# The receptance weights of the first unit split into two parts, with another written order of the work

## The chip, the cores and the metric

The kernel runs on one core of a Trainium2 chip. The core has five engines that run at the same time, each through its own queue in order: PE (matrix multiplication), DVE (vector), ACT (scalar functions), POOL (GpSimd) and SP, which here issues the transfers. The metric is the device time of one execution in microseconds (us). The kernel before takes 607.31 us, the median of three runs (607.2 to 607.88).

## The reference

Two layers. The first is causal attention in a window: 8 batches, 8 heads, 576 tokens, 64 values a head; each token sees itself and the 63 tokens before it. Its output x (8 x 576 x 512) goes into the second layer:

```
x_prev = x moved by one token
xk = mu_k * x + (1 - mu_k) * x_prev
xr = mu_r * x + (1 - mu_r) * x_prev
k  = relu(xk @ w_k)                       # 512 x 1024
v  = (k * k) @ w_v                        # 1024 x 512
r  = 1 / (1 + exp(-(xr @ w_r)))           # 512 x 512
out = r * v
```

All tensors come as 64-bit numbers for the weights and 32-bit for the rest; the result is 32-bit.

## The kernel before, in words

**Units.** The 4608 tokens are cut into NU = 9 units of 512 tokens. Each unit runs through attention (`scores`, `soften`, `flip`, `values`), the mixes `xr` and `xk` (function `mix`), and the three products (`r_units`, `k_units`, `v_units`). The features of x stand on the partitions in NC = 4 chunks c of 128.

**Two ways to multiply.** A 32-bit factor is either kept whole, and a product is one 32-bit matmul of `xm` with `whole`; or it is split into a high part (a rounded copy) and a low part (the rest, a subtraction), and a product is three faster matmuls: high by high, high by low, low by high, of `xs` with `ws`. The function `direct` decides by the letters in `DIRECT`, and only for the first unit (u = 0): with "rk" the products with w_r and w_k are whole there. All other units, and w_v always, use the split factors. So the split of w_r and w_k is needed anyway, but before only from the second unit on.

**Weights.** `decode` turns each piece of 128 x 512 weights (n = 0 to 3 are w_r) from two 32-bit words into one 32-bit number: `sign` (ACT), `clamp` (POOL or DVE), `shift`, `top` and `low` (DVE). The result is a tile `wt` or, where it is used whole, half of a pair tile `whole`. `first_part` writes the high part `ws[:, 0]` (ACT or POOL), `second_part` subtracts and writes the low part `ws[:, 1]` (POOL or DVE).

**Mixes.** `mix` makes one chunk of xr or xk: `diff` (a scaled x_prev, on ACT, POOL or DVE), `blend` (DVE) and, where the factor is split, `high` (ACT or POOL) and `low` (POOL or DVE). The pieces that are whole write to a tile `xm`; the split ones have a scratch tile `d` and a tile `xs`.

**The order.** Every step is a `Piece` with a number. `play` plans which piece runs next on which engine. The table `ORDER` gives, for each of PE, DVE, ACT, POOL and SP, the numbers of the first pieces in the order in which the engine runs them; the rest follows by keys. While the planner's clock is under `BOUND`, a piece on POOL is also tied to the last DVE piece marked `port` that the planner started before it: the POOL instruction then waits on a semaphore until that DVE instruction is done (`Engine.behind`, `add_manual_dep` with the reason "port"). Nearly all instructions are issued by one helper, `issue`, so the profile has line L168 for them.

**Attention in the head of the program.** The first unit's attention goes in groups of two tiles `pr`. The scores are multiplied (`qk` or `qks`), the probabilities `pr` are made by DVE and ACT, multiplied by the reciprocal row sums `rs` on POOL or DVE, turned by PE (matmul with `ident`, called a flip, four to a tile), copied to `pt`, and multiplied with `v`. Two such groups give one chunk xT of x, from which `mix` works.

Of the kernel before, what the change touches and what calls it, by code (L numbers as in the profile page):

```python
# [47 lines left out]
GATES = 1  # L48
LATER = (4,)

DIRECT = "rk"
SPLIT = (-9, -47)
WHOLE = 859

# [34 lines left out]

ORDER = {  # L90
    "PE": (
        509, 510, 535, 531, 566, 533, 559, 561, 557, 555, 590, 563, 1502, 1509, 1516, 1523, 588, 586, 645, 614,
        1503, 1510, 612, 1524, 1517, 610, 667, 616, 1511, 1525, 1518, 1504, 1505, 1526, 1512, 1519, 1530, 1531,
        1538, 1532, 1539, 1540, 1546, 1547, 1554, 1533, 1548, 1541, 720, 1562, 1555, 1556, 1570, 1549, 1563, 1571,
        1557, 1564, 742, 1578, 1586, 1579, 1572, 1565, 1580, 1581, 1594, 1587, 1588, 689, 690, 1573, 1589, 1595,
        1604, 1596, 1614, 1605, 1624, 1625, 1626, 1615, 1606, 1607, 764, 765, 1597, 1598, 1627, 1599, 1616, 1628,
        1617, 1608, 1609, 1600, 1618, 771, 793, 1619, 1620, 1629, 1610, 1630, 1621, 1601, 1611, 1631, 1674, 1680,
        1681, 1682, 1686, 1675, 1692, 1676, 1677, 1683, 1693, 1698, 1694, 1706, 1695, 1707, 1708, 1714, 1709, 1715,
        1716, 1699, 1717, 1722, 1723, 1730, 1724,
    ),  # L100
    "DVE": (
        6, 7, 511, 513, 517, 521, 515, 525, 527, 523, 519, 8, 9, 529, 544, 536, 548, 540, 538, 550, 546, 542, 19,
        532, 20, 552, 567, 554, 575, 571, 581, 579, 577, 569, 573, 40, 21, 1487, 599, 591, 605, 31, 595, 593, 601,
        583, 32, 603, 597, 584, 33, 589, 1489, 23, 607, 646, 654, 648, 48, 658, 660, 49, 656, 650, 50, 652, 64, 55,
        65, 1491, 668, 66, 674, 56, 57, 676, 1493, 1495, 58, 72, 1497, 88, 662, 89, 682, 90, 1499, 73, 74, 80, 672,
        81, 680, 82, 678, 96, 104, 1501, 1508, 105, 670, 106, 1529, 97, 119, 98, 1522, 120, 664, 1515, 121, 666,
        122, 1537, 721, 128, 112, 729, 727, 113, 725, 731, 114, 733, 723, 735, 129, 684, 60, 130, 136, 137, 138,
        686, 144, 743, 747, 688, 1561, 745, 751, 145, 749, 146, 753, 757, 755, 100, 737, 52, 1553, 691, 152, 153,
        692, 159, 1569, 160, 738, 759, 739, 154, 161, 763, 162, 156, 741, 761, 164, 1635, 1585, 1593, 766, 168, 769,
        169, 170, 176, 767, 1640, 177, 1645, 84, 1650, 178, 772, 1655, 778, 794, 780, 782, 784, 802, 786, 808, 1648,  # L110
        180, 776, 806, 796, 1660, 774, 800, 1602, 804, 1612, 1632, 76, 1653, 1670, 1665, 1622, 798, 788, 1673, 1668,
        792, 1685, 790, 810, 813, 811, 814, 812, 1679, 1697,
    ),
    "ACT": (
        5, 514, 518, 512, 516, 522, 526, 524, 528, 17, 545, 537, 541, 539, 549, 547, 551, 543, 534, 29, 560, 562,
        582, 558, 556, 574, 576, 568, 570, 572, 580, 578, 600, 564, 602, 592, 598, 604, 606, 594, 587, 596, 46, 615,
        62, 655, 54, 34, 649, 613, 651, 659, 611, 661, 647, 70, 617, 657, 86, 1494, 78, 1496, 653, 1498, 94, 59,
        102, 1527, 1506, 1520, 677, 1528, 669, 673, 1507, 1513, 683, 118, 1521, 671, 126, 1534, 1514, 1535, 1542,
        110, 1536, 1543, 679, 1544, 681, 123, 134, 675, 142, 728, 1550, 730, 107, 732, 1558, 150, 1551, 99, 1559,
        131, 139, 1552, 726, 1560, 722, 1566, 724, 736, 1582, 744, 750, 746, 734, 147, 75, 1583, 758, 748, 158,  # L120
        1567, 756, 1568, 754, 693, 752, 1574, 1584, 1590, 694, 1575, 1591, 155, 166, 1576, 163, 1592, 1634, 174,
        1639, 768, 1644, 1649, 1654, 1651, 1646, 115, 179, 1642, 1647, 803, 1656, 773, 783, 785, 1664, 1669, 781,
        1657, 807, 775, 805, 777, 795, 801, 779, 787, 1671, 797, 1667, 1672, 799, 809, 1678, 1684, 1696, 1710, 1718,
        1719,
    ),
    "POOL": (
        643, 520, 10, 18, 530, 553, 30, 565, 1486, 644, 585, 1488, 22, 47, 609, 608, 63, 618, 1490, 51, 11, 1492,
        71, 87, 79, 95, 665, 35, 663, 1500, 103, 67, 68, 127, 83, 91, 111, 124, 1545, 135, 685, 143, 687, 151, 132,
        140, 108, 740, 695, 148, 762, 760, 167, 1577, 1636, 770, 175, 1637, 171, 172, 1638, 1641, 92, 1659, 1652,
        116, 1661, 1643, 1666, 1662, 1658, 789, 791, 1663, 1711,  # L130
    ),
    "SP": (
        4, 1, 0, 2, 3, 12, 13, 16, 38, 25, 27, 39, 24, 15, 14, 28, 631, 633, 41, 42, 26, 43, 619, 44, 620, 634, 622,
        621, 632, 45, 61, 53, 36, 37, 69, 85, 639, 77, 93, 101, 709, 696, 708, 701, 641, 711, 125, 640, 117, 700,
        624, 703, 705, 630, 699, 623, 173, 628, 698, 697, 710, 625, 704, 109, 165, 141, 133, 636, 642, 702, 635,
        706, 149, 157, 638, 626, 707, 629, 627, 637, 182, 719, 716, 181, 713, 196, 203, 718, 715, 712, 195, 714,
        717, 193, 198, 183, 199, 184, 185, 192, 201, 202, 194, 234, 204, 200, 219, 218, 191, 1603, 208, 187, 189,
        206, 188, 220, 207, 186, 1613, 197, 190, 1623,
    ),
}  # L140

# [6 lines left out]
def attn_rwkv_kernel(ctx, tc, qT, kT, v2, mu_k, mu_r, w_k, w_v, w_r, out):  # L148
# [335 lines left out]
    def direct(ws, u):  # L484
        return u == 0 and any(ws is a and nm in DIRECT for nm, a in (("r", wr_s), ("k", wk_s), ("v", wv_s)))

# [723 lines left out]
```

## Time and profile before

| | |
|---|---|
| median of three runs | 607.31 us |
| the profiled execution | 607.59 us |
| its span, first to last instruction | 605.8 us (1.8 us lie outside) |
| PE busy | 593.6 us, 98% |
| DVE, ACT, POOL busy | 65%, 61%, 22% |

The busy share of PE says how much of the span it has an instruction in work. The spans of instructions that follow each other in PE overlap by a little, so the time that a group costs is read from the start of one row to the start of the next.

### The profile page before, as it was taken

The page shows a single profiled execution, that of the slowest core. Times are in us where ns is not written, and L with a number is a line of the kernel's source. Part 1 is how long each engine was busy: PE and PEld are TensorE (multiplying, and loading weights), DVE is VectorE, ACT ScalarE, POOL GpSimd, SP SyncE. Part 2 cuts the span into 40 slices and gives each one's busy share as a digit, 9 for nine tenths or more (in the row PEclk, how much of TensorE's full clock was granted, in tenths as well). Part 3 has the DMA queues.
Part 4 walks back from the last instruction along what each step waited for, and adds up shares of the span by engine and source line. Part 5 has one row for each costly group of instructions (what it writes and reads, how often), then busy time and mean ns, then how long its engine had stood idle before and what let it go on. Part 6 is the DMA issues. An engine that isn't in the chain of part 4 may idle for free.

```text
span 605.8 us, 17561 instructions
## 1 busy us (share of the span) xinstructions
PE 593.6 (98%) x7008; PEld 464.7 (77%) x7008; DVE 391.1 (65%) x1210; ACT 371.3 (61%) x1057; POOL 133.9 (22%) x205
## 2 busy tenths in 40 slices
PE   5999999999999999999999999999999999999997
PEld 4644577888888888888888888887888888888885
DVE  5999999737782768366754677277828683665211
ACT  6898967475576646673577358645865476743620
POOL 6665546202300330022101130023002300201000
PEclk9999999999999999999999999999999999999999
DMA  8988133213221323122312222132212220010001
GB/s 276 320 287 282 47 88 105 80 45 107 83 77 46 93 75 97 40 82 63 110 40 57 88 83 66 41 110 81 75 46 93 92 81 24 3 53 18 0 18 52
DMA packets 56913, 53.32 MB, mean 88 GB/s; under 512 B 10496, under 2 KB 50432, under 8 KB 56832
## 3 DMA queue, kind: packets, MB, share of 16 engines
q1 hardware_dynamic: 56832, 52.20, 28.2%
q8 instruction: 56, 0.92, 0.6%
q14 instruction: 25, 0.20, 0.1%
HBM read 42.73 MB, written 9.44 MB: 86 GB/s over the span
## 4 chain that ended last, share of the span: by engine, by line
PE 84%; DVE 6%; ACT 4%; DMA 3%; SPq 1%; issue 1%; POOL 1%; ACTq 0%
PE bank L168 84%; DVE bank L168 1%; DMA raw<-w_k 1%; ACT pr L168 1%; SPq L168 1%; DMA v<-v 1%; DMA raw<-w_r 1%; DVE xm L168 1%; ACT ws L168 1%; DVE wt L168 1%; ACT kf L168 1%; DVE d L168 1%; DVE r L168 0%; DVE whole L168 0%; DVE pt L168 0%
## 5 line engine op out<-in xcount | busy, mean ns | idle before, releaser
L168 PE MATMUL bank<-xs,ws 128*128 128x512 f32 x1152 | 272.7, 396 | 0.0
L168 PEld LDWEIGHTS bank<-xs,ws 128*128 128x128 f32 x1152 | 215.8, 188 | 51.0
L168 PE MATMUL bank<-ks,ws 128*128 128x512 f32 x864 | 206.8, 398 | 0.1
L168 PEld LDWEIGHTS bank<-ks,ws 128*128 128x128 f32 x864 | 161.3, 188 | 39.5 <-issue 1.0
L168 DVE TENSOR_TENSOR ks<-kf,ks 128x512 fp32r<-128x512 f32 x70 | 51.3, 734 | 93.7 <-ACT ks L168 93.5
L168 ACT ACTIVATE pr<-pr,nmax 128x96 f32<-128x96 f32 (+1 forms) x288 | 105.2, 368 | 8.8 <-DVE nmax L168 8.3
L168 ACT ACTIVATE kf<-bank 128x512 f32<-128x512 f32 x72 | 43.0, 598 | 61.1 <-PE bank L168 60.7
L168 DVE CUSTOM_DVE_ANT_0 pr<-bank,bands 128x96 f32<-128x96 f32 x256 | 49.5, 250 | 14.3 <-PE bank L168 14.3
L168 POOL CAST ks<-kf 128x512 fp32r<-128x512 f32 x7 | 4.3, 612 | 244.9 <-ACT kf L168 206.0
L168 ACT COPY xT<-bank 128x256 f32<-128x256 f32 (+1 forms) x43 | 14.5, 392 | 67.0 <-PE bank L168 67.0
L168 ACT ACTIVATION_READ_ACCUMULATOR pr<-pr,nmax 128x1 f32 x288 | 54.5, 189 | 0.0
L168 ACT ACTIVATE kf<-kf 128x512 f32<-128x512 f32 x71 | 44.8, 633 | 2.0
L168 ACT ACTIVATE th<-bank 128x512 f32<-128x512 f32 x36 | 21.3, 591 | 38.5 <-PE bank L168 27.2
L168 DVE SCALAR_TENSOR_TENSOR r<-bank,r 128x512 f32<-128x512 f32 x36 | 24.4, 680 | 31.4 <-PE bank L168 31.3
L168 PE MATMUL bank<-xm,whole 128*128 128x512 f32 x96 | 43.1, 599 | 0.0
L168 ACT CAST ks<-kf 128x512 fp32r<-128x512 f32 x65 | 40.3, 620 | 2.1 <-POOL kf L168 0.3
L168 PE MATMUL bank<-qk 64*32 64x96 f32 (+1 forms) x2112 | 33.4, 254 | 7.8 <-DMA qk<-kT 5.2
L168 PEld LDWEIGHTS bank<-qk 64*32 64x32 f32 (+1 forms) x2112 | 28.2, 108 | 15.9 <-DMA qk<-qT 5.2
L168 PEld LDWEIGHTS bank<-pt,v 32*64 32x64 f32 (+1 forms) x2656 | 34.3, 130 | 7.0 <-issue 5.0
L168 ACT CAST xs<-d 128x512 fp32r<-128x512 f32 x49 | 28.8, 618 | 15.3 <-POOL d L168 13.7
L168 DVE TENSOR_TENSOR xs<-d,xs 128x512 fp32r<-128x512 f32 x57 | 37.3, 698 | 0.4 <-ACT xs L168 0.4
L168 DVE COPY xT<-bank 128x256 f32<-128x256 f32 x26 | 10.3, 421 | 42.2 <-PE bank L168 42.2
(79 smaller groups left out, 562.0 us busy)
## 6 DMA issues: line engine op xcount, KB each, us to landing
v<-v SPq DMA_DIRECT2D x68, 64.0 KB, 2.0
raw<-w_k SPq DMA_DIRECT2D x8, 512.0 KB, 8.4
raw<-w_v SPq DMA_DIRECT2D x8, 512.0 KB, 6.0
v<-v SPq DMA_DIRECT2D x60, 48.0 KB, 2.0
raw<-w_r SPq DMA_DIRECT2D x4, 512.0 KB, 4.8
outT<-r SPq DMA_DIRECT2D x8, 256.0 KB, 2.0
v<-v SPq DMA_DIRECT2D x60, 32.0 KB, 1.9
qk<-kT SPq DMA_DIRECT2D x8, 224.0 KB, 3.7
```

The costliest lines, as they stand in the source:

```text
L168: self.last = tc.keep_in_program_order(op(*args, **kw))
```

## The change

`DIRECT` loses its "r": in the first unit, the products with w_r now use split factors, as in all other units. The four chunks of `xr` of that unit each get a high and a low part (4 more copies, 4 more subtractions), and the 16 products with w_r become 48 matmuls instead of 16. The product with w_k stays whole there. The table `ORDER` is a new one, with more pieces in it; the waits of POOL come by the same rule as before.

```diff
-DIRECT = "rk"
+DIRECT = "k"
 SPLIT = (-9, -47)
 WHOLE = 859
...
 ORDER = {
     "PE": (
-        509, 510, 535, 531, 566, 533, 559, 561, 557, 555, 590, 563, 1502, 1509, 1516, 1523, 588, 586, 645, 614,
...
+        509, 510, 535, 531, 533, 566, 559, 561, 555, 557, 590, 563, 588, 1510, 1517, 586, 1524, 645, 614, 1531, 612,
...
```

The new table has two lines more, so line L168 of the profile is L170 in the changed kernel. The three pieces below show how the order stands, word for word, in the program before and in the changed one.

PE at the head of the program, before. `ident,pr` are flips, `xm,whole` are whole products with w_r:

```order
L168 MATMUL bank<-ident,pr 128x128 x4
L168 MATMUL bank<-qks 64x128 x16
L168 MATMUL bank<-ident,pr 128x128 x4
L168 MATMUL bank<-pt,v 64x64 x16
L168 MATMUL bank<-ident,pr 128x128 x8
L168 MATMUL bank<-qks 64x128 x16
L168 MATMUL bank<-pt,v 64x64 x16
L168 MATMUL bank<-xm,whole 128x512 x4
L168 MATMUL bank<-ident,pr 128x128 x8
L168 MATMUL bank<-qk 32x96 x32
L168 MATMUL bank<-pt,v 64x64 x16
L168 MATMUL bank<-xm,whole 128x512 x2
```

The same place now; three matmuls of `xs,ws` are one product with w_r (`ws_253` is the first piece of w_r, `ws_333` the second):

```order
L170 MATMUL bank<-ident,pr 128x128 x8
L170 MATMUL bank<-qks 64x128 x16
L170 MATMUL bank<-pt,v 64x64 x16
L170 MATMUL bank<-ident,pr 128x128 x8
L170 MATMUL bank<-qks 64x128 x16
L170 MATMUL bank<-pt,v 64x64 x16
L170 MATMUL bank<-ident,pr 128x128 x4
L170 MATMUL bank<-xs,ws_253 128x512 x6
L170 MATMUL bank<-ident,pr 128x128 x4
L170 MATMUL bank<-xs,ws_253 128x512 x3
L170 MATMUL bank<-qk 32x96 x32
L170 MATMUL bank<-pt,v 64x64 x16
```

Both flips of the first group stand ahead of the next scores `qks`, and one more block of four flips stands ahead of the first product with w_r.

POOL at the head, before. `pr` are the scaled probabilities, `wt` the clamps, `xm_395` the scaled x_prev of the first chunk of xr:

```order
L168 TENSOR_TENSOR pr_186<-pr_186,rs_189 128x512
L168 CAST ws0_251<-whole_236 128x512
L168 TENSOR_SCALAR wt_240<-wt_240 128x512
L168 TENSOR_TENSOR pr_195<-pr_195,rs_198 128x512
L168 TENSOR_TENSOR pr_258<-pr_258,rs_256 128x512
L168 TENSOR_SCALAR wt_336<-wt_336 128x512
L168 MEMSET xT_350 128x2
L168 TENSOR_SCALAR xm_395<-xT_350,mu1_116 128x512
L168 COPY bands00_440<-bands_117 128x96
```

The same place now; `d_408` takes the part of `xm_395`, and `ws0_253` and `xs_407` are the subtractions that make the low parts of w_r's first piece and of xr's first chunk:

```order
L170 TENSOR_TENSOR pr_186<-pr_186,rs_189 128x512
L170 CAST ws0_253<-wt_155 128x512
L170 TENSOR_SCALAR wt_246<-wt_246 128x512
L170 TENSOR_TENSOR pr_197<-pr_197,rs_200 128x512
L170 TENSOR_TENSOR ws0_253<-wt_155,ws0_253 128x512
L170 TENSOR_SCALAR wt_274<-wt_274 128x512
L170 TENSOR_TENSOR pr_255<-pr_255,rs_258 128x512
L170 TENSOR_TENSOR pr_260<-pr_260,rs_258 128x512
L170 MEMSET xT_358 128x2
L170 TENSOR_SCALAR d_408<-xT_358,mu1_116 128x512
L170 TENSOR_TENSOR pr_340<-pr_340,rs_338 128x512
L170 TENSOR_TENSOR xs_407<-d_408,xs_407 128x512
```

One subtraction of weights and one multiplication of probabilities stand ahead of the scaled x_prev that did not before, and a multiplication and a subtraction stand between it and the first product with w_r.

PE from the last attention block of the first unit to the first products with w_k, before:

```order
L168 MATMUL bank<-qk 32x96 x32
L168 MATMUL bank<-pt,vs 64x64 x16
L168 MATMUL bank<-xm,whole 128x512 x20
L168 MATMUL bank<-qk 32x96 x32
L168 MATMUL bank<-xm,whole 128x512 x9
```

And now:

```order
L170 MATMUL bank<-qk 32x96 x32
L170 MATMUL bank<-pt,vs 64x64 x16
L170 MATMUL bank<-xs,ws_333 128x512 x6
L170 MATMUL bank<-xs,ws_583 128x512 x12
L170 MATMUL bank<-xs,ws_720 128x512 x12
L170 MATMUL bank<-xm,whole 128x512 x23
L170 MATMUL bank<-qk 32x96 x32
```

Before, 8 of the 20 whole products were with w_r and 12 with w_k; now ten split products with w_r are followed by 23 whole ones with w_k.

## Rows read from the trace of the kernel before

**Rows 1.** The page: busy time, share and instructions of each engine.

```profile
PE 593.6 (98%) x7008; PEld 464.7 (77%) x7008; DVE 391.1 (65%) x1210; ACT 371.3 (61%) x1057; POOL 133.9 (22%) x205
```

**Rows 2.** The chain that ended last, from 90 us: start, length, what.

```profile
92.80 509.43 PE bank L168 x4956
```

**Rows 3.** Timeline of PE, 0 to 106 us: start, length, work, idle before.

```profile
11.04 1.11 PE L168 MATMUL bank<-ident,pr 128*128 128x128 f32 x4
...
14.20 0.66 PE L168 MATMUL bank<-ident,pr 128*128 128x128 f32 x4
...
19.84 3.70 PE L168 MATMUL bank<-xm,whole 128*128 128x512 f32 x8
...
28.17 0.61 PE L168 MATMUL bank<-ident,pr 128*128 128x128 f32 x4
28.62 1.88 PE L168 MATMUL bank<-xm,whole 128*128 128x512 f32 x4
30.34 0.60 PE L168 MATMUL bank<-ident,pr 128*128 128x128 f32 x4
31.17 1.00 PE L168 MATMUL bank<-qk 64*32 64x96 f32 x64 [0.23 <-ACT pt L168]
32.36 1.15 PE L168 MATMUL bank<-pt,vs 128*64 128x64 f32 x32 [0.20 <-ACT pt L168]
33.44 17.43 PE L168 MATMUL bank<-xm,whole 128*128 128x512 f32 x40
...
60.21 0.99 PE L168 MATMUL bank<-qk 64*32 64x96 f32 x64 [0.48 <-ACT kf L168]
...
92.80 0.97 PE L168 MATMUL bank<-qk 64*32 64x96 f32 x62 [0.28 <-DVE wt L168]
```

**Rows 4.** Timeline of PE, 100 to 150 us.

```profile
100.07 22.48 PE L168 MATMUL bank<-xs,ws 128*128 128x512 f32 x96
122.48 2.06 PE L168 MATMUL bank<-pt,v 32*64 32x96 f32 x160
```

**Rows 5.** Stretches: length, busy time (instructions) by engine, granted clock, DMA share, GB/s.

```profile
10.00:20.00 10.00, 9.46 (x168) 7.56 (x162) 9.18 (x52) 9.01 (x36) 5.04 (x9) 1.00 1.01 338
20.00:40.00 20.00, 19.57 (x240) 11.02 (x241) 19.13 (x65) 18.48 (x59) 12.72 (x22) 1.00 0.94 316
40.00:60.00 20.00, 19.73 (x108) 8.63 (x106) 19.46 (x56) 17.67 (x46) 11.92 (x15) 1.00 0.86 268
60.00:80.00 20.00, 19.79 (x277) 12.72 (x278) 19.02 (x51) 19.55 (x60) 10.44 (x12) 1.00 0.25 68
80.00:100.00 20.00, 19.67 (x355) 15.54 (x354) 19.03 (x56) 12.80 (x35) 12.38 (x16) 1.00 0.22 56
```

**Rows 6.** Timeline of POOL, 5 to 36 us.

```profile
10.82 0.61 POOL L168 CAST ws<-whole 128x512 fp32r<-128x512 f32 x1 [0.45 <-DVE rs L168]
11.52 0.61 POOL L168 TENSOR_SCALAR wt<-wt 128x512 f32<-128x512 f32 x1
16.04 1.04 POOL L168 TENSOR_TENSOR pr<-pr,rs 128x512 f32<-128x512 f32 x1 [2.90 <-DVE pr L168]
```

**Rows 7.** Groups of instructions: count, busy us, mean ns of one, idle before.

```profile
L168 DVE TENSOR_TENSOR xs<-d,xs 128x512 fp32r<-128x512 f32 x57 | 37.3, 698 | 0.4 <-ACT xs L168 0.4
L168 POOL TENSOR_TENSOR xs<-d,xs 128x512 fp32r<-128x512 f32 x7 | 9.5, 1354 | 22.0 <-ACT xs L168 19.7 <-DVE d L168 1.9 <-DVE rs L168 0.4
L168 POOL TENSOR_TENSOR ws<-whole,ws 128x512 fp32r<-128x512 f32 x6 | 7.7, 1285 | 4.2 <-DVE r L168 1.6 <-DVE bank L168 1.2 <-ACT d L168 0.7
L168 POOL TENSOR_SCALAR xm<-xT,mu 128x512 f32<-128x512 f32 x5 | 3.5, 696 | 2.0 <-ACT xT L168 0.8 <-DVE pr L168 0.7 <-DVE mu L168 0.2
```

**Rows 8.** Timeline of POOL and of DVE, 75.6 to 80 us.

```profile
77.15 0.83 POOL L168 TENSOR_TENSOR pr<-pr,rs 128x384 f32<-128x384 f32 x1 [2.74 <-DVE pt L168]
...
77.47 1.05 DVE L168 SCALAR_TENSOR_TENSOR bank<-raw,wt 128x512 uint32<-128x512 uint32 x1
78.45 0.56 DVE L168 STREAM_TRANSPOSE pt<-pr 128x384 f32<-128x384 f32 x1
```

## What the change will do

> **What bounds the kernel now.** I read the page first: PE is busy for 593.6 of 605.8 us, the next engine, DVE, for 391.1 [rows 1]. Then the end of the chain of waits: from 92.80 on, 509.43 us of PE alone lead to the end [rows 2], and what PE waited for at 92.80 is a DVE instruction that decodes weights [rows 3]. So the end of the program is PE's work, plus what PE waits before about 93 us; whatever the change saves or costs there is seen in full at the end, and nothing after it can hide it. Third, PE's timeline. The first product with w_r starts at 19.84 and the first product with w_k at 33.44 + 0.10 + 8 x 0.86 = 40.41 (8 of the 20 products in that row are with w_r) [rows 3]. After that PE waits 0.48 us at 60.21 and 0.28 at 92.80 [rows 3]. Last, the stretches: between 20 and 100 us DVE is busy 95% and more, and between 60 and 80 ACT is at 19.55 of 20 [rows 5]. PE is the bound, but its feeders have little to spare.
>
> **What it saves.** Two whole products take 1.72 us (28.62 to 30.34), 0.86 each [rows 3]; 32 split products take 122.48 - 100.07 = 22.41 with the change to the next kind of work, 0.70 each [rows 3, 4]. For 16 products that is 16 x (0.86 - 0.70) = 2.6 us less work for PE. In PE's count of instructions it looks the other way (48 matmuls instead of 16), but the durations decide.
>
> **What it adds.** Four copies (0.6 us each on ACT or POOL) and four subtractions of xr's parts; a subtraction is 0.70 us on DVE and 1.35 on POOL [rows 7]. By engine the changed program has 3 instructions more on ACT, 2 on DVE and 3 on POOL. On DVE that is 2 x 0.6 = 1.2 to 1.4 us in a stretch that has 80 - 19.13 - 19.46 - 19.02 - 19.03 = 3.4 us free between 20 and 100 [rows 5]. It fits, but a third of the slack is gone.
>
> **What it moves, and this decides.** Before, the first product with w_r needed one number ready, the whole xm and the whole weights. Now it also needs the low part of the weights and the low part of xr's first chunk, and the new order gives both to POOL. So I followed POOL through its head with the durations of its rows.
> The first multiplication of probabilities ends, and the cast of ws0 waits for a DVE reciprocal as it did before (10.82, [rows 6]); in the new order that reciprocal comes a little later, about 11.1. Cast to 11.8 (10.82 to 11.52 is 0.70), clamp to 12.4, multiplication by rs to 13.4 (1.0), low part of ws0 to 14.7 (1.29), the next clamp to 15.3 [rows 6, 7]. Then POOL waits for DVE's reciprocal of the second group, which I get at 16.05: DVE takes up its shift of wt_246 when the clamp is done, and scores, shift and copy up to there are 3.3 us of its instructions. Two multiplications to 18.1. The scaled x_prev d_408 then is tied to DVE's low part of ws1, at about 19.2 by the same count; 0.7 for it [rows 7], 19.9. DVE's blend to 20.7. POOL, in its order, puts the multiplication pr_340 next, tied to the blend: 21.1 to 22.1, and then the low part xs_407 of 1.35: **23.45**. PE gets its first complete product at about 23.5, where before it was 19.84 [rows 3].
> From there PE needs 16 x 0.70 = 11.1 us of products and the attention work that stood between them. Before, 19.84 to 40.41 was 20.57 us, of which 16 x 0.86 = 13.7 were products; of the 6.8 that are left, one block of flips (0.45, 28.17 to 28.62 [rows 3]) now comes earlier and 0.43 were waits for ACT (31.17 and 32.36 [rows 3]). That leaves 6.0, and 23.5 + 11.1 + 6.0 = 40.6 at the earliest. The operands are close behind each other there: the low part of xr's third chunk about 35.0 for a need at 35.3, that of the fourth about 38.3 for a need at 38.1. I take 0.2 to 0.6 for that: the first product with w_k at 40.8 to 41.2, that is **0.4 to 0.8 us later** than before. The 2.6 us saved are eaten by 3.6 us of later start, less 0.9 of work brought forward or waits that end.
>
> **After 41 us.** From here the same products with w_k follow. DVE has its operands 1.4 to 1.7 us ahead by my count (the whole weights that are needed at 53.0 are there at 51.3), POOL's low parts of w_k and w_v 1.2 to 1.7 us. PE's old waits (0.48 + 0.28 and a short one at about 86, some 0.8 us in all [rows 3]) should mostly vanish, since the order is another and PE comes later; new ones may come where the second unit's xr is made on POOL, with a margin of only 0.6 to 0.8 us. I take -0.8 to 0 for the old, 0 to +0.8 for the new, and -0.4 for both.
> The sum: +0.6 - 0.4 = +0.2, between 0.4 - 0.8 = -0.4 and 0.8 + 0.8 = +1.6. On the profiled execution's 607.59 that is 607.8; it stands 0.28 over the median of the runs, so 607.31 + 0.2 = **607.5**.
>
> **What POOL's waits are worth.** At 77.47 a DVE instruction that reads two operands from SBUF takes 0.98 us (next start 78.45) while POOL's multiplication runs from 77.15 to 77.98; its neighbours take 0.5 to 0.6 [rows 8]. So work on both engines at once is not free, and a wait in POOL costs less than its length. I price the tie at what POOL waits, and nothing for the DVE instruction that is spared. The Trainium skill ("SBUF — State Buffer", section "SBUF: two separate sides") says that a DVE instruction with two SBUF inputs and a GpSimd instruction that reads SBUF take an exclusive lock for the whole instruction, the loser fully blocked; the 0.98 agrees in kind. By that rule the ties lose nothing that the lock wouldn't take, so the sum stays what it is with them; without them the added subtractions would block DVE for as long.
>
> **Rivals.**
> *The gain stays.* If the walk through POOL is too slow by 1 us at two of its four ties (my times for DVE there are counted, not seen), the first product is complete at about 21.5. Then PE reaches w_k at 38.6 + 0.2, 1.6 us earlier, and with 0.4 to 0.8 of old waits gone the end is 605.1. For it: POOL is busy only 5.04 of 10 us there [rows 5], and the chain is mostly ties. Against it: then the fourth chunk's low part (38.3) is the next bound, with DVE at 95%, and takes back most. 605.1.
> *GpSimd comes too late (the other side).* POOL feeds the second chunk of xr too: after 23.45 a clamp, a multiplication, the masks' copies, a multiplication, then xs_502's low part, at 28.7, needed at about 29.8. One more wait of the kind that POOL has at 16.04 (2.90 us for DVE [rows 6]) on that way puts it at 31.6, and PE stands for 1.8. This decides from 29.8 on. All later multiplications on POOL, and so the flips, move with it. 607.5 + 1.8 = 609.3.
> *PE's clock.* The same four flips took 1.11 us at 11.04 and 0.66 at 14.20, after PE had worked nearly without a pause from 9 us on [rows 3]; from 10 us on the granted clock is 1.00 in all stretches [rows 5], the upper level, 2.4 GHz. In the new order PE waits ahead of the scores, since both flips of the first group come first, and again from about 19.7 to 23.5. If the first 4 us of products ran at the pace of those first flips, they would take 4 x (1 - 0.66/1.11) = 1.6 us more: 609.1. The Trainium skill ("TensorE: Matmul & The Clock Gate", section "Part 1: The HAM clock gate") says that idle gaps send the array back to 1.2 GHz; the slow first flips agree, and no row of before shows a fall after the rise.
> *DVE or ACT late in the second unit.* The 1.2 to 1.4 us more on DVE and three copies (1.8 us) more on ACT, which has 0.45 us free between 60 and 80 [rows 5], come out at its operands: up to 1.4 us, 608.9.
>
> **How the numbers follow.** What one can tell from no change here is 0.2%, 1.2 us: 606.1 to 608.5. The forecast of 607.5 with its own range 606.9 to 608.9 gets 0.45; the gain that stays 0.22; GpSimd late 0.19; the clock 0.07; DVE or ACT late in the second unit 0.07. Within 0.2% lie 0.38 of the forecast, 0.04 of the gain (where it is smaller) and 0.03 of the last rival: 0.45. Faster: 0.18 of the gain and 0.05 of the forecast's low side, 0.23. Slower: 0.19, 0.07, 0.04 of the last and 0.02 of the forecast's high side, 0.32. The range that leaves out 2 in 10 goes from 605.0 to 610.0: below the gain's 605.1, above GpSimd's 609.3 with some more of the same.
>
> **What would show it.** In the profile after: the first split product with w_r at about 23.5 with an idle of 3 us or more before it, released by POOL's low part of xs; the first whole product with w_k at 40.8 to 41.2; PE's work less by about 2.6 us and its waits before 41 more by about as much; the wait at 60.21 gone or shorter. Wrong would be: the first product with w_r at 21.5 or earlier, w_k's first at 39 (the gain stays), a wait of over 1 us ahead of the second chunk's products with a POOL instruction as releaser (GpSimd), flips or products in the head that take 1.7 times as long (clock), or a wait between 80 and 110 us of over 0.8 (second unit).

## The result, and the profile after

The changed kernel takes 611.2 us, the median of five runs (610.5 to 613.61), against 607.6 for the kernel before: ratio 1.0068, 95% interval 1.0051 to 1.0085. It is slower, where no change was forecast. Three of the five runs lie at 610.5 to 611.2 with a mean granted clock of 1.00, two, of which there is no trace, at 613.0 and 613.6 with 0.991. The profiled execution took 610.5 us, its span 608.7, that is 2.9 more than before; the account below is of these 2.9, and not of the 3.6 between the medians.

The page of the changed kernel, engines (answers to [rows 1]):

```profile
PE 592.2 (97%) x7024; PEld 467.9 (77%) x7024; DVE 390.5 (64%) x1212; ACT 372.3 (61%) x1060; POOL 136.2 (22%) x208
```

PE is busy for 1.4 us less than before, and the span is longer: PE waits more. Its timeline, as in [rows 3] and [rows 4]:

```profile
10.83 1.12 PE L170 MATMUL bank<-ident,pr 128*128 128x128 f32 x4 [1.02 <-POOL pr L170]
13.84 1.11 PE L170 MATMUL bank<-ident,pr 128*128 128x128 f32 x4 [1.89 <-POOL pr L170]
14.88 1.99 PE L170 MATMUL bank<-qks 64*64 64x128 f32 x32
...
23.92 0.48 PE L170 MATMUL bank<-xs,ws 128*128 128x512 f32 x1
24.74 1.43 PE L170 MATMUL bank<-xs,ws 128*128 128x512 f32 x5 [0.34 <-POOL xs L170]
...
34.90 7.32 PE L170 MATMUL bank<-xs,ws 128*128 128x512 f32 x30
42.05 19.91 PE L170 MATMUL bank<-xm,whole 128*128 128x512 f32 x46
...
78.88 2.21 PE L170 MATMUL bank<-pt,v 32*64 32x96 f32 x160
81.02 0.73 PE L170 MATMUL bank<-ks,ws 128*128 128x512 f32 x2
82.47 12.94 PE L170 MATMUL bank<-ks,ws 128*128 128x512 f32 x55 [0.72 <-issue]
95.34 2.06 PE L170 MATMUL bank<-pt,v 32*64 32x96 f32 x160
97.33 1.33 PE L170 MATMUL bank<-qk 64*32 64x96 f32 x92
99.94 0.73 PE L170 MATMUL bank<-qk 64*32 64x96 f32 x36 [1.28 <-issue]
```

The first complete product with w_r goes on at 24.74, when POOL's low part of xs is there. The first product with w_k starts at 42.05 instead of 40.41, so **1.64 us** are lost by then. The rest is in two waits that were not in the forecast, 0.72 and 1.28 us, **2.00 us** together, which the profile puts down to "issue": PE waited for nothing that it shows. The waits of 0.48 and 0.28 us at 60.21 and 92.80 [rows 3] are gone. 1.64 + 2.00 - 0.76 = 2.88: that is the 2.9 us of the span. The end of the chain says the same, with no feeder in it any more (answers to [rows 2]):

```profile
59.82 21.93 PE bank L170 x284
81.75 0.72 issue
82.47 16.19 PE bank L170 x247
98.66 1.28 issue
99.94 505.20 PE bank L170 x4930
```

How POOL came to 24.74, from the timelines of POOL and of DVE (answers to [rows 6]):

```profile
20.10 0.69 POOL L170 TENSOR_SCALAR d<-xT,mu 128x512 f32<-128x512 f32 x1 [1.63 <-DVE ws L170]
22.41 1.04 POOL L170 TENSOR_TENSOR pr<-pr,rs 128x512 f32<-128x512 f32 x1 [1.63 <-DVE nmax L170]
23.41 1.27 POOL L170 TENSOR_TENSOR xs<-d,xs 128x512 fp32r<-128x512 f32 x1
```

```profile
16.92 0.29 DVE L170 CUSTOM_DVE_ANT_0 pr<-bank,mask 128x128 f32<-128x128 f32 x1 [0.68 <-PE bank L170]
...
19.20 0.69 DVE L170 TENSOR_TENSOR ws<-wt,ws 128x512 fp32r<-128x512 f32 x1
```

Two things are late ahead of this. POOL's clamp started at 12.16, after 0.33 us of waiting for ACT, which had waited until 11.39 for its load of w_r; the chain that ended last begins with this load. And DVE stood 0.68 us for PE's scores, which had started at 14.88 and took 1.99 where those at 19.12 take 1.10; what stands behind them on DVE, and POOL that is tied to it, is late with them. What each of the two costs is told at e3_best.

### The profile page after: what moved, and what is told of

Its sections match the earlier page's. It is cut to its first block, busy times and chain, and to the rows that moved or that the text cites. A ratio compares the mean times of both kernels' runs of the same rounds, so it can differ in the third digit from the quotient of the medians.

```text
span 608.7 us, 17609 instructions
## 1 busy us (share of the span) xinstructions
PE 592.2 (97%) x7024; PEld 467.9 (77%) x7024; DVE 390.5 (64%) x1212; ACT 372.3 (61%) x1060; POOL 136.2 (22%) x208
## 4 chain that ended last, share of the span: by engine, by line
PE 95%; DMA 2%; POOL 1%; DVE 1%; issue 0%; ACT 0%; SPq 0%; POOLq 0%
PE bank L170 95%; DMA raw<-w_r 2%; POOL pr L170 1%; DVE pr L170 0%; POOL xs L170 0%; POOL wt L170 0%; DVE d L170 0%; POOL d L170 0%; DVE r L170 0%; ACT wt L170 0%; DVE ws L170 0%; DVE bank L170 0%; SPq L170 0%; DVE rs L170 0%; DVE nmax L170 0%
## 5 line engine op out<-in xcount | busy, mean ns | idle before, releaser
L170 PE MATMUL bank<-xs,ws 128*128 128x512 f32 x1200 | 285.9, 396 | 0.3 <-POOL xs L170 0.3
L170 PEld LDWEIGHTS bank<-xs,ws 128*128 128x128 f32 x1200 | 224.2, 188 | 53.9 <-POOL xs L170 0.7
L170 PE MATMUL bank<-ks,ws 128*128 128x512 f32 x864 | 206.8, 397 | 0.7 <-issue 0.7
L170 PEld LDWEIGHTS bank<-ks,ws 128*128 128x128 f32 x864 | 161.4, 188 | 40.1 <-issue 1.6
L170 ACT ACTIVATE pr<-pr,nmax 128x96 f32<-128x96 f32 (+1 forms) x288 | 104.9, 366 | 14.8 <-DVE nmax L170 14.3
L170 DVE TENSOR_TENSOR ks<-kf,ks 128x512 fp32r<-128x512 f32 x70 | 50.5, 723 | 96.7 <-ACT ks L170 96.2
L170 ACT ACTIVATE kf<-bank 128x512 f32<-128x512 f32 x72 | 42.8, 597 | 63.9 <-PE bank L170 63.7
L170 DVE CUSTOM_DVE_ANT_0 pr<-bank,bands 128x96 f32<-128x96 f32 x256 | 49.4, 250 | 16.8 <-PE bank L170 16.8
L170 POOL CAST ks<-kf 128x512 fp32r<-128x512 f32 x8 | 4.9, 611 | 234.1 <-ACT kf L170 195.1
L170 ACT COPY xT<-bank 128x256 f32<-128x256 f32 (+1 forms) x43 | 14.4, 389 | 67.2 <-PE bank L170 67.2
L170 ACT ACTIVATION_READ_ACCUMULATOR pr<-pr,nmax 128x1 f32 x288 | 54.0, 188 | 0.0
L170 ACT ACTIVATE kf<-kf 128x512 f32<-128x512 f32 x71 | 44.7, 630 | 2.1
L170 DVE SCALAR_TENSOR_TENSOR r<-bank,r 128x512 f32<-128x512 f32 x36 | 24.5, 682 | 31.1 <-PE bank L170 31.0
L170 ACT ACTIVATE th<-bank 128x512 f32<-128x512 f32 x36 | 21.2, 590 | 33.5 <-PE bank L170 22.5
L170 PEld LDWEIGHTS bank<-pt,v 32*64 32x64 f32 (+1 forms) x2656 | 34.8, 130 | 7.8 <-issue 6.4
L170 ACT CAST ks<-kf 128x512 fp32r<-128x512 f32 x64 | 39.4, 619 | 1.8
L170 PE MATMUL bank<-qk 64*32 64x96 f32 (+1 forms) x2112 | 33.4, 254 | 6.9 <-DMA qk<-qT 5.3
L170 ACT CAST xs<-d 128x512 fp32r<-128x512 f32 x51 | 30.4, 617 | 15.3 <-POOL d L170 13.6
L170 PEld LDWEIGHTS bank<-qk 64*32 64x32 f32 (+1 forms) x2112 | 28.2, 108 | 14.2 <-issue 5.6
L170 DVE TENSOR_TENSOR xs<-d,xs 128x512 fp32r<-128x512 f32 x58 | 37.4, 684 | 2.7 <-POOL xs L170 1.8
L170 PE MATMUL bank<-pt,v 32*64 32x96 f32 (+3 forms) x2656 | 37.1, 244 | 1.1 <-ACT pt L170 0.7
L170 DVE COPY xT<-bank 128x256 f32<-128x256 f32 (+1 forms) x26 | 10.5, 431 | 39.8 <-PE bank L170 39.7
```

The lines of the kernel that those rows point to most:

```text
L170: self.last = tc.keep_in_program_order(op(*args, **kw))
```

## The experiments

All ratios are to the kernel before, run beside; the changed kernel's is 1.0068. Theory A is that the two waits for "issue" are PE waiting for its own instructions; B that POOL's waits made the change slow; C that PE's clock did; D that DVE's order holds back the second unit's xr.

### Where the 2.0 us of "issue" come from

**e1_place2**: one alignment more. An instruction takes one slot in the stream of its engine. In the kernel, `values` asks for some groups to start at slot 7 of a block of 256 slots (`addr_align`, line 666 before).

```diff
-PLACES, SKIP = {3: 7, 4: 7, 8: 7, 12: 7, 16: 7}, 12
+PLACES, SKIP = {2: 7, 3: 7, 4: 7, 8: 7, 12: 7, 16: 7}, 12
```

> The changed kernel with one address alignment more: the first values of the second unit (at 78.88) start at slot 7 of a block of 256 instruction slots, as later ones do. No work and no order is changed. Theory A: the wait of 0.72 us at 81.75 goes or moves to another place in the block (249 slots into the values instead of after them) and the span falls by up to 0.7 us; the wait in the scores stays at 1.1 to 1.4 us. Rival (a data wait): 0.72 us stays where it is, right behind the first matmuls with w_v.

Ratio 1.0045 (1.003 to 1.006; this interval and the changed kernel's overlap). PE's timeline in it:

```profile
78.70 2.21 PE L170 MATMUL bank<-pt,v 32*64 32x96 f32 x160
80.84 13.53 PE L170 MATMUL bank<-ks,ws 128*128 128x512 f32 x57
94.31 2.06 PE L170 MATMUL bank<-pt,v 32*64 32x96 f32 x160
96.30 1.33 PE L170 MATMUL bank<-qk 64*32 64x96 f32 x92
99.39 0.73 PE L170 MATMUL bank<-qk 64*32 64x96 f32 x36 [1.76 <-issue]
```

The wait at 81 is gone with no instruction moved, so it was no wait for data. The one in the scores grew from 1.28 to 1.76, so only part of the 0.72 was won: the products behind the scores start at 100.05 instead of 100.60, and of these 0.55 us the span shows 0.2 (608.5).

**e2_off71**: besides, the second such group at slot 71 instead of 7.

```diff
-PLACES, SKIP = {3: 7, 4: 7, 8: 7, 12: 7, 16: 7}, 12
+PLACES, SKIP = {2: 7, 3: 71, 4: 7, 8: 7, 12: 7, 16: 7}, 12
```

> The changed kernel with two alignments: the first values of the second unit at slot 7 of a block, and the next ones (at about 94.3) at slot 71 instead of 7. No work and no order is changed. Theory A (blocks of 256 instruction slots): 441 slots of small matmuls fit into the rest of that block and the next, 320 of the values and 121 of the scores, four to a score; so PE's wait moves from the 46th score (92 matmul records) to the 30th or 31st (60 to 62 records), and no wait at 81. Rival (a data wait in the scores): it stays at 92 records. Time 608.5 to 610.5.

Ratio 1.0042 (1.0027 to 1.0057).

```profile
97.10 0.96 PE L170 MATMUL bank<-qk 64*32 64x96 f32 x60
99.57 1.06 PE L170 MATMUL bank<-qk 64*32 64x96 f32 x68 [1.50 <-issue]
```

The wait moved from the 92nd to the 60th record of the scores. Each record has a weight load beside it, so the values are 320 slots, and 320 + 2 x 60 = 440 is what fits from slot 71 to the end of the next block (441); in the changed kernel it was 320 + 2 x 92 = 504, from slot 7 (505). Both ends lie at the same place, the end of the second block. Theory A is shown: PE stops at the boundary of a block of 256 slots. The trace of the transfers has one of 16 KB on queue q8, "instruction", for each: in the changed kernel it starts at 97.72 (one packet between 97.6 and 97.8), and PE goes on at 99.94.

```profile
q8 instruction: 1, 0.02, 33.3%
```

In the changed kernel and the eight runs with such a wait between 79 and 105 us, PE went on 2.2 to 2.8 us after such a transfer had started. Values and scores back to back use up a block in 1.6 to 1.9 us (160 values take 1.99, 92 scores 1.33).

**e1_apart**: three products between values and scores.

```diff
-        1637, 1608, 1628, 1629, 1616, 1638, 1639, 1609, 764, 765, 771, 793, 1682, 1688, 1683, 1694, 1689, 1617,
-        1618, 1619, 1690, ...
+        1637, 1608, 1628, 1629, 1616, 1638, 1639, 1609, 764, 765, 1617, 1618, 1619, 771, 793, 1682, 1688, 1683, 1694, 1689,
+        1690, ...
```

> The changed kernel with three products (9 matmuls with w_v, 2.1 us) moved on PE from behind the scores of the second half of the second unit to between the values and these scores, so that 320 + 256 instruction slots of small matmuls no longer follow each other. Theory A (instruction blocks): the wait of 1.28 us in the middle of the scores is gone, the one of 0.72 at 81.75 stays, the span falls by 1.0 to 1.3 us to 607.4 to 607.7. Rival (a data wait, the same inputs being late): PE waits as long at another place and the span stays at 608.5 or more.

Ratio 1.007 (1.0055 to 1.0085), a miss in time: the wait in the scores was gone as expected (128 records in one piece), the one at 81 was 1.09, and PE then stood 0.92 for POOL's xs at 106.46. The 1.28 us had been hiding a late feeder: 0.37 more at 81 and 0.92 at 106 make up for it.

### What is late behind it

**e2_split**: e1_place2, and the three products between the two groups of scores (`764, 765, 771, 1617, 1618, 1619, 793`).

> The changed kernel with the alignment at 81 and, on PE, three products with w_v (2.1 us) moved from behind the two groups of scores to between them; the first group follows the values at once as before. Theory A: 320 + 128 slots of small matmuls, then 9 slow ones: both waits for instructions are gone, and DVE has the first scores as early as before, so the wait of 0.9 us for POOL's xs that came with the products ahead of both groups is smaller. Span 606.8 to 607.5, ratio to the kernel before 1.001 to 1.003. Rival (the feeders are late anyway, and the waits for instructions only hid it): PE waits 1 us or more for xs between 100 and 110 us, span 608 or more.

Ratio 1.0051 (1.0035 to 1.0066). No wait for instructions was left between 40 and 110 us, but PE's timeline has the rival:

```profile
106.20 2.36 PE L170 MATMUL bank<-xs,ws 128*128 128x512 f32 x9 [0.92 <-POOL xs L170]
109.15 3.05 PE L170 MATMUL bank<-xs,ws 128*128 128x512 f32 x12 [0.58 <-POOL xs L170]
```

And DVE's timeline the cause:

```profile
101.39 0.26 DVE L170 CUSTOM_DVE_ANT_0 pr<-bank,bands 128x96 f32<-128x96 f32 x1 [3.38 <-PE bank L170]
...
101.58 1.41 DVE L170 SCALAR_TENSOR_TENSOR d<-xT,mur,d 128x512 f32<-128x512 f32 x2
```

DVE stands idle for 3.38 us on a maximum of the second group's scores, with two blends of the second unit's xr behind it.

**e3_blend**: e2_split with that maximum (802) behind the blends (1653, 1658), and slot 160 instead of 7 for the group at 79.

```diff
-        170, 172, 762, 1643, 1648, 741, 763, 761, 1651, 1630, 1610, 1640, 84, 768, 767, 802, 1653, 1658, 806, 772,
+        170, 172, 762, 1643, 1648, 741, 763, 761, 1651, 1630, 1610, 1640, 84, 768, 767, 1653, 1658, 802, 806, 772,
```

> The changed kernel with the values of the second unit at slot 160 of a block at 79 us, the three products between the two groups of scores as in e2_split, and on DVE one maximum (802, of the second group) behind the two blends that stood behind it. Theory D (once PE no longer waits for instructions, what is late is xr of the third chunk of the second unit, because DVE's blends stand behind a maximum that waits for the second group's scores; DVE was idle for 2.5 us there): the blends start at about 98 to 99 instead of 101, PE's waits for POOL's xs of 0.92 and 0.58 us at 106 and 109 are gone or under 0.3, span 607.0 to 608.0, ratio 1.001 to 1.004. Rival (POOL itself is late): the waits stay at 0.7 us or more, span 608.5 or more.

Ratio 1.0029 (1.002 to 1.0038), span 606.0: theory D holds. The blends start at 98.08, and PE waits for nothing between 42 and 112 us:

```profile
41.69 19.91 PE L170 MATMUL bank<-xm,whole 128*128 128x512 f32 x46
...
100.41 11.89 PE L170 MATMUL bank<-xs,ws 128*128 128x512 f32 x50
```

**e4_blend_only**: the changed kernel with that move alone (802 behind 1653 and 1658).

> The changed kernel with one maximum on DVE moved behind two blends (the last part of e3_blend alone); PE's order and the alignments are as in the changed kernel. If the waits for instructions alone set the time between 80 and 110 us, nothing is won: both stay (0.6 to 1.3 us at about 81 and 98) and the time is that of the changed kernel, 610.5 to 611.5, ratio 1.006 to 1.008. If the blends cost beside them: ratio 1.004 or less.

Ratio 1.0086 (1.0064 to 1.0108): nothing is won; PE waited 1.01 and 1.54 us for its instructions. The blends count only once the instructions are in time.

### The head: clock and POOL

**e1_flipback**: the scores ahead of the second flips again.

```diff
-        509, 510, 535, 531, 533, 566, 559, ...
+        509, 510, 535, 531, 566, 533, 559, ...
```

> The changed kernel with one place of PE's order as before: the scores of the third tile ahead of the second flips of the first (scores at about 12, not at 14.88). If the order of PE in the head costs time by idling (theory C, the clock and the late scores), the scores and flips up to 18 us come earlier by 1 to 2 us, flips run at 0.66 us instead of 1.11 at about 14, and w_k's first whole product comes 0.3 to 1.0 us earlier than 42.05. If POOL alone sets the head (theory B), w_k's first product stays at 41.8 to 42.1.

Ratio 1.0088 (1.0068 to 1.0108), a miss: the scores waited 2.41 us for their q (its load stands where the new order of SP has it) and started at 14.05; w_k's first product came at 43.30. In this execution the granted clock was 0.52 between 13.2 and 20.1 us, so the run tells little of theory C.

**e2_warm**: e2_split with 19 idle matmuls on PE, 8 ahead of the first scores, 4 and 7 ahead of the first two blocks of flips. Their results are overwritten.

```diff
+WARM = {(0, 0): 4, (0, 1): 7}
...
+    def warm(count, ps):
+        for _ in range(count):
+            pe.matmul(ps, ident, ident, start=True, stop=True)
...
+        warm(8 if g == 0 and half == 0 else 0, banks[g, half][0][:, 0] if half is not None else None)
...
+        warm(WARM[g, h] if (g, h) in WARM else 0, ps[:, 0])
```

> e2_split with 19 idle matmuls of the identity on PE in the head, which write to banks that are overwritten: 8 ahead of the first scores, 4 and 7 ahead of the first two blocks of flips, where PE waits for POOL. Theory C (PE's pauses in the head keep its clock at 1.2 GHz for 3 us longer than before): flips at 14 take 0.66 us instead of 1.11, scores after them 1.1 instead of 1.99, the first whole product with w_k comes 0.5 to 1.2 us earlier than in e2_split, time 0.5 to 1.2 us less, and no execution with a mean clock of 0.99. Rival (POOL and DVE set the head alone): w_k's first product within 0.2 us of e2_split's.

Ratio 1.0061 (1.0042 to 1.008). The head did what was expected: the flips at 13.31 took 0.65, the scores at 13.90 1.10, and w_k's first product came at 41.24 (the changed kernel 42.05; e2_split 42.71, in an execution with a mean granted clock of 0.994). The time did not fall: PE waited 0.92 us for POOL's xs at 106.13 as in e2_split, and 1.20 us for issue at 80.99, though that group stands at slot 7 as in e2_split, where it did not wait:

```profile
78.03 1.76 PE L171 MATMUL bank<-pt,v 32*64 32x96 f32 x123
80.99 0.71 PE L171 MATMUL bank<-pt,v 32*64 32x96 f32 x37 [1.20 <-issue]
```

The wait stands behind 123 records, 246 slots from slot 7: the end of the first block. The transfer for the next block started at 78.60, 0.6 us behind the start of the values, and PE went on 2.4 us after it; in e2_split it had started at 77.34, 2.2 us ahead of its values. So this too is a block that came late. Why its transfer started later in one kernel than in the other stays open.

**e2_bwarm**: the kernel before with 12 such matmuls (8 and 4), and the alignment.

> The kernel before with 12 such idle matmuls (8 ahead of the first scores, 4 ahead of the first flips) and the alignment of the first values of the second unit. Theory C: the flips at 11.04 and the scores at 12.30 run at the upper clock, but the first product with w_r at 19.84 waits for DVE's blend, so little is gained: w_k's first product at 39.9 to 40.4 instead of 40.41, ratio 0.9985 to 1.0005. Rival (the clock sets the head of before too): w_k's first product a whole us or more earlier, ratio 0.998 or less.

Ratio 1.000 (0.999 to 1.001). The flips did not run at the upper clock: they came at 11.97, behind idle matmuls of 2.07 us, and took 1.06, with a granted clock of 0.51 between 9.6 and 13.1 us. The scores at 12.96 took 1.13, and w_k's first product came at 39.6 (32.64 + 0.10 + 8 x 0.86), 0.8 earlier, a little more than expected. No time came of it: PE was 1.0 us ahead where the second unit's products with xs start (99.07, before 100.07), but the span was shorter by 0.3 only; the rest was lost later, without a wait, in groups that each took a few hundredths longer. So what is won in the head of the kernel before did not come out at its end.

**e3_low**: the low part of xr's first chunk on DVE (piece 1489 from POOL's row to DVE's).

```diff
-        643, 520, 10, 18, 530, 11, 30, 553, 554, 565, 1486, 585, 1489, 47, 584, ...
+        643, 520, 10, 18, 530, 11, 30, 553, 554, 565, 1486, 585, 47, 584, ...
```

> The changed kernel with one subtraction moved: the low part of xr's first chunk (xs_407) from POOL to DVE, behind five of the eight maxima of the next scores. Theory (POOL's chain in the head, with the subtraction of 1.27 us behind a multiplication at 22.41, sets the first complete product with w_r): the second matmul with w_r starts at 23.0 to 23.9 instead of 24.74, and POOL's next multiplication and so the next flips come a microsecond earlier; w_k's first whole product at 41.2 to 41.7 instead of 42.05. Rival (the flips and DVE set it): 24.4 or later, w_k's first product at 42 or later.

Ratio 1.0081 (1.0067 to 1.0095). Its profiled execution had a granted clock of 0.59 between 23 and 27 us (w_k's first product at 43.38), so its trace decides nothing; but two of its executions had a granted clock of 1.00, and at 611.4 and 612.2 us they were no faster than the changed kernel.

**e3_best**: e3_blend and e2_warm together.

> e3_blend with the 19 idle matmuls of e2_warm in the head. If the two gains add up (the clock 0.8 us at w_k's first product, as e2_warm showed, the blends about 1 us): w_k's first product at 41.2, no wait of over 0.5 us between 79 and 110, span 606.2 to 607.2, ratio 0.999 to 1.002. If the feeders of the second unit set the time anyway, what is won in the head is waited for there: span 608 or more.

Ratio 1.0005 (0.9996 to 1.0014): the whole loss is back, and nothing beyond it. PE's timeline:

```profile
14.04 1.10 PE L171 MATMUL bank<-qks 64*64 64x128 f32 x32
...
23.54 1.44 PE L171 MATMUL bank<-xs,ws 128*128 128x512 f32 x5 [0.34 <-POOL xs L171]
...
40.87 19.91 PE L171 MATMUL bank<-xm,whole 128*128 128x512 f32 x46
```

The span is 605.2, shorter than expected. With the clock up, the first complete product is at 23.54 and w_k's first at 40.87. The idle matmuls are all that e3_blend and e3_best differ in. On POOL the two multiplications of the second group start at 16.04 and 16.00, the scaled x_prev behind them, tied to DVE, at 19.74 and 18.90; w_k's first product stands at 41.69 and 40.87. So the clock costs 0.8 us here, and the medians fall by 1.2 (608.4 to 607.2). The changed kernel's 42.05 is 0.36 later than e3_blend's 41.69, with the same order up to there: its clamp on POOL, which waited for the load of w_r, started at 12.16, that of e3_blend at 11.81 without a wait. The 1.64 us of the head are thus 0.46 of e3_best, 0.82 of the clock and 0.36 of the load; the last differs from one execution to the next.

**e4_best_low**: e3_best with e3_low's move.

> e3_best with the low part of xr's first chunk on DVE instead of POOL. If POOL's chain sets the first complete product with w_r once the clock is up: its second matmul at 22.9 to 23.2 instead of 23.54, w_k's first whole product 0.3 to 1.0 us earlier than 40.87, ratio 0.998 to 1.0. If the flips and the later operands set it: w_k's first product within 0.2 us of 40.87 or later, ratio 1.0 or more.

Ratio 1.0022 (1.0012 to 1.0032), slower than e3_best. The second matmul came at once (six in one row from 22.99, no wait for xs), but w_k's first product came at 42.31, a miss: PE waited 1.41 us for ACT's pt at 28.52. On DVE the moved subtraction stands in the way:

```profile
21.83 1.24 DVE L171 TENSOR_TENSOR xs<-d,xs 128x512 fp32r<-128x512 f32 x1 [0.27 <-ACT xs L171]
```

It runs beside POOL's multiplication at 21.48 and takes 1.24 us, and it stands behind three of the eight maxima, not five. The fourth starts at 22.99 (21.20 in e3_best); ACT stood 1.12 us for it, and its copy of pt came at 27.91 (26.13). POOL lost as well: its multiplication at 28.69 waited 2.67 us for a DVE instruction, where e3_best had it at 27.15 without a wait. DVE paid more than POOL was spared.

### POOL's waits

**e1_noties**, and **e3_bnoties** the same in the kernel before:

```diff
-BOUND = 125000
+BOUND = 0
```

> The changed kernel and its order with all waits of POOL for DVE's last instruction taken out (the instructions and their order stay). Theory A (the two waits of 0.72 us at 81.75 and 1.28 us at 98.66 that the profile of the changed kernel puts down to issue are PE waiting for its own next block of instructions): both stay within 0.2 us, and only the head moves. Rival B (POOL's waits are what made the change slow): POOL's 1.6 us waits at 18.5 and 20.8 go, the first whole product with w_k starts at 40.5 or earlier instead of 42.05, and the span falls from 608.7 to 607 or less. By theory A alone the span stays above 607.5.

> The kernel before with all waits of POOL for DVE's last instruction taken out. If these waits pay for themselves because work on both engines at once lengthens both (in the changed kernel without them, DVE's blends of xr took 998 ns instead of 749, POOL's scaled x_prev 1054 instead of 693): slower, ratio 1.003 to 1.01. If they only cost: faster, ratio 0.999 or less.

Ratios 1.0153 (1.0137 to 1.0169) and 1.0053 (1.0039 to 1.0067): theory B falls. Without the waits, 10 to 62 us, in the changed kernel first with and then without them, DVE's blends and POOL's scaled x_prev:

```profile
L170 DVE SCALAR_TENSOR_TENSOR d<-xT,mur,d 128x512 f32<-128x512 f32 x4 | 3.0, 749 | 0.7 <-POOL d L170 0.5 <-ACT d L170 0.2
...
L170 POOL TENSOR_SCALAR d<-xT,mu 128x512 f32<-128x512 f32 x2 | 1.4, 693 | 3.1 <-DVE ws L170 1.6 <-DVE nmax L170 1.4
```

```profile
L170 DVE SCALAR_TENSOR_TENSOR d<-xT,mur,d 128x512 f32<-128x512 f32 x4 | 4.0, 998 | 0.2 <-ACT d L170 0.2
...
L170 POOL TENSOR_SCALAR d<-xT,mu 128x512 f32<-128x512 f32 x2 | 2.1, 1054 | 3.1 <-issue 2.2 <-ACT xT L170 0.9
```

Both engines lose, DVE 0.25 us a blend, and DVE is what PE then waits for (2.0 us for a whole weight at 63.91 in the one, 2.2 at 45.13 in the other). In e1_noties the head came 0.85 us earlier as far as 23.89, and all of it and more was lost by 45. The clock also falls in both traces after it had risen; in e1_noties here:

```profile
8.40:11.90 3.50, 1.68 (x32) 1.20 (x24) 3.43 (x18) 3.06 (x15) 2.04 (x3) 1.00 0.92 332
11.90:18.70 6.80, 5.57 (x72) 4.79 (x73) 6.29 (x36) 6.32 (x28) 5.08 (x7) 0.53 1.02 372
```

But this is not e1_noties' loss: an execution of it with a granted clock of 1.000 took 615.6 us, the profiled one, with 0.994, 615.9. In e3_bnoties the clock does count. Behind the wait at 45.13 it was 0.50 from 46.3 to 49.7, and the 18 matmuls from 45.13 on took 9.69 us, where 40 of the same kind take 17.37 in the kernel before, 0.43 each (7.8 for 18). Its one execution with 1.000 took 608.8 us, those with 0.997 took 610.3 to 610.7, the kernel before 606.8: about half of the 0.5% is the clock, and the rest stays.

## Why the prediction was wrong

**The bound** was read rightly: PE sets the end, and the changed kernel's waits ahead of 100 us are seen in full there (2.88 of 2.9 us). It is not so for each microsecond: 0.3 of 1.0 was left in e2_bwarm, 0.2 of 0.55 in e1_place2.

**The saving** of 2.6 us: ten products from 34.90 to 42.05 are 0.715 each, so 16 x (0.86 - 0.715) = 2.3. Right for the products; PE's busy time on the page fell by 1.4 only.

**POOL's walk through the head** ended at 23.45 for the low part xs_407, and put w_k's first product at 40.8 to 41.2, 0.4 to 0.8 late. The changed kernel had 24.68 and 42.05, 1.64 late; e3_best, with PE's clock up, 23.48 (POOL's 22.21 + 1.27) and 40.87. The walk thus counted right for a PE at 2.4 GHz, step by step within about 0.3 us; that it ends within 0.03 is luck. What failed in it is that it took PE's scores as in time: at the lower level they took 1.99 us, at the upper 1.10, and that is 0.8 us. Another 0.36 is the load of w_r, for which the walk has no wait.

**The rival on the clock** named the right pauses, those ahead of the scores, but priced the wrong work. The products that it thought slow ran at the upper level (five in 1.43 us at 24.74); the flips and scores before them were slow. Its price is also miscounted: 4 us of products at the pace 1.11 to 0.66 take 4 x (1.11 / 0.66 - 1) = 2.7 us more, not 1.6. Measured are 0.8. And it stood as an alternative with 0.07, where it was an addition to the forecast. It leaned on a granted clock of 1.00 from 10 us on [rows 5], which misled: the clock records of a trace begin with the first rise, at 13.96 us in the kernel before, 17.30 in the changed one, 18.51 in e3_blend and 4.38 in e3_best. A stretch ahead of that reads 1.00 for want of a record, and the level is told by the durations (the scores at 12.30 took 1.97).

**After 41 us** I set -0.4 for old waits that vanish and new ones. The old went (-0.76), no operand of w_k or of the second unit was late in the changed kernel: the margins of 0.6 to 1.7 us held. But 2.00 us came from PE's own instructions, for which the sum has nothing. This is the step that failed most: a term of 0 to +0.8 for new waits was 2.00, of a kind that was not in it. The argument followed every operand and not the instruction stream, though PE's order of the changed kernel has the values and both groups of scores back to back, where the kernel before had eleven products between, and though the kernel aligns these very groups by hand. The Trainium skill ("Runtime: NRT & Kernel Launch", section "Instruction fetch mechanics") says that an engine's instructions come in blocks of 16 KiB, 256 instructions, the next fetched while one runs; the waits at the 60th and the 92nd record, and at the 123rd in e2_warm, agree with the size. It calls the cost mostly hidden; here it was 0.72 and 1.28 us.

**The other rivals.** The gain did not stay: the first product was later, not earlier, than walked. GpSimd late for the second chunk did not happen: POOL's xs_502 ended at 30.6, and PE has no wait ahead of these products. The second unit's operands were not late as long as PE waited for instructions; with these in time they were (e2_split), by DVE's order and not for want of DVE's time. Two of the signs for a wrong forecast did show, the slow flips (1.11 us at 13.84) and a wait of over 0.8 us between 80 and 110, the second for another reason than the sign was meant for.

**What POOL's waits are worth** I priced at what POOL waits, with nothing for what they spare. In this the sign was wrong: taking them out costs 0.5% in the kernel before, about half of it by the clock, and 0.85% more in the changed one. That the collisions of DVE and POOL are the reason is seen in the longer instructions and in PE's waits for DVE; no run separates them from the changed order in time.

## What to carry to other kernels

Where PE is the bound and its order is rewritten, count its instructions between slow ones as well as its operands: values and scores back to back used up a block of instructions in 1.6 to 1.9 us while the next took 2.2 to 2.8 to come. A wait taken away may only uncover the next: the time came back when instructions, DVE's order and the clock were all mended (e3_best). Of these, the alignment alone brought little (1.0045 against 1.0068) and DVE's order alone nothing (1.0086); the clock alone was not tried in the changed kernel. Rivals that can hold together belong into the sum as terms, not side by side with a chance each.

## What the runs showed of the hardware

PE's wait for its instructions stands in the profile as "issue", with no releaser, in the middle of a group of alike matmuls; it moved from record 92 to record 60 with the alignment alone, and 16 KB transfers on the instruction queue start 2.2 to 2.8 us before it ends. PE's clock rose once and fell again within the first 20 us in e1_noties (1.00 until 11.9, 0.53 until 18.7), while PE stood for POOL, 1.17 us ahead of the flips at 10.59 and 1.89 ahead of those at 13.13. In the changed kernel 32 scores take 1.99 us at 14.88 and 1.10 at 19.12, though the profile reads a granted clock of 1.00 for both: it has no clock record ahead of the first rise. With the ties of POOL to DVE out, both engines' instructions are longer, 693 to 1054 ns (two of POOL) and 749 to 998 (four of DVE).
